# Issuing the stores of P's 16-bit planes from GpSimd's queue

## The chip, the cores and the metric

The kernel runs on one NeuronCore of a Trainium2 chip. The core has five instruction streams that run side by side and meet only at semaphores: TensorE (PE in the profile) multiplies matrices, VectorE (DVE), ScalarE (ACT) and GpSimd (POOL) work on tiles of up to 128 partitions, and SyncE (SP) only issues transfers. Transfers (DMAs) run on 16 DMA engines of the core; an instruction in the queue of SP, ACT or POOL starts one. Each stream takes its instructions strictly in order, so an instruction that waits holds everything behind it in the same stream.

The metric is the time of one execution in microseconds on the device; a kernel's figure is the median of several runs.

## The reference

The inputs are q, k and v of shape (8, 8, 576, 64) and two weight matrices of 512 x 2048 and 2048 x 512. The reference is top-32 attention, then a Fourier mixing block with a small network:

```
scores = (q @ k^T) / 8                       # 64 heads of 576 x 576
kth    = 32nd largest score of each row
P      = softmax(scores where scores >= kth, else -1e9)
x      = P @ v, heads side by side           # (8, 576, 512)
u      = x + real(fft(fft(x, axis=1), axis=2))
un     = (u - mean(u)) / sqrt(var(u) + 1e-6) # over the 512 channels
out    = u + relu(un @ w_ch1) @ w_ch2
```

Everything is computed in float32.

## The kernel before

Heads are taken in 32 pairs, four pairs to each of the 8 batches. The scores of a pair are cut into nine tiles of at most 128 query rows by 576 keys (`IN_PAIR`): four blocks of 128 rows for each of the two heads, and one tile that holds the last 64 rows of both. That makes 288 tiles. The program is written out by hand, one step for each tile i, in the loop at the end of the kernel; there is no scheduler that reorders it. In a step, each engine's instructions for several tiles stand together:

- Scores of tile i + 3: TensorE multiplies (L371 to L404), ScalarE copies them from PSUM to an SBUF tile S, of which there are six.
- The 32 largest scores per row of tile i: VectorE takes four rounds of "eight largest" (MAX8, L425) with three rounds of "replace them" (MATCH_REPLACE8, L427) into a tile wk (`Wk`). A first half of tile i + 1's rounds is mixed in.
- The bound of tile i (`bounds`, L434): one small multiplication on GpSimd writes nt, the negated row maximum and the scaled threshold.
- The mask of tile i - 1 (`mask`, L448 and L451): ScalarE writes a huge number into wk wherever a score lies below the threshold, then GpSimd subtracts this from the scores. The mask needs nt, the subtraction needs the mask.
- The exponential of tile i - 1 (`expo`, L459) on ScalarE.

P @ v needs P with keys on the partitions, that is, transposed. In the first batch, in pair 7 and in the last pair TensorE transposes P (`transposes`, L527). In the other 26 pairs, 234 tiles (`by_dma`), it is done by DMA. There ScalarE writes the exponential into S, and then, two steps after the tile's own, `plane` lets ScalarE split the float32 words into two planes of 16 bits, low halves and high halves (L472, two copies into wk). The planes are stored to a DRAM tile `planes` (L485; for the 64 + 64 row tile two stores, L488). There are 208 stores of 128 rows and 52 of 64 rows. In the next step `turn` (L506) loads the planes back through a transposing DMA into PT, issued by SP; one such load covers a block of both heads. One step after the load's step come the 20 matmuls of P @ v for a chunk of query rows (`attend`, L564), which need all transposing loads of the chunk. Tile wk comes from a pool of three pairs of buffers and is free for a new tile when its store has been read.

Between these, a queue of units of the Fourier block and of the network (`mlp_units`) fills TensorE's time: the matmuls at L755, L812, L816, L966, L993, L1032 and L1163. Around it GpSimd also does the folds ahead of the Fourier step (L651, L678, L719), additions (L839, L1022, L1135) and sums of the network's hidden tiles (L1108). SP also loads q, k and v for coming pairs (L240 to L288), the parts of W2 (L909), and writes the results (L1002, L1059, L1142). The order in each of these streams is that of the program text: in a step `turn`, then the mask, then `plane`, then the units, the loads, the bound, and the rest.

Of the kernel before, what the change touches and what calls it, by code (L numbers as in the profile page):

```python
# [73 lines left out]
def kernel(  # L74
# [9 lines left out]
    nc = tc.nc  # L84
    B, H, S, D = q.shape
# [356 lines left out]
    def by_dma(i):  # L442
        return pair_by_dma(i // PER_PAIR)
# [22 lines left out]
    def plane(i, half):  # L466

        if not (0 <= i < N and by_dma(i)):
            return
        words = Wk[i].bitcast(U16).rearrange("p (h s) -> p h s", h=2)  # L470
        src = Ssb[i].bitcast(U16).rearrange("p (s h) -> p h s", h=2)
        nc.scalar.copy(out=words[:, half, :], in_=src[:, half, :])  # L472
        if half == 0:
            return
        Ssb.pop(i)
        Wk.pop(i)
        pair, t, e = items[i]
        nq = TAIL if e is None else P
        if e != 1:
            planes_of[pair, t] = dramp.tile(  # L480
                [nq, 2, 2 * S], U16, name=f"planes_{pair}_{t}", tag="planes", bufs=3
            )
        to = planes_of[pair, t]
        if e is not None:
            nc.sync.dma_start(out=to[:, :, S * e:S * (e + 1)], in_=words)  # L485
        else:
            for h in range(2):
                nc.sync.dma_start(  # L488
                    out=to[:, :, S * h:S * (h + 1)], in_=words[nq * h:nq * (h + 1)]
                )  # L490
        if e != 1:
            Wp.pop(i)
# [879 lines left out]
    for o, place in ((B12, w2_12), (B21, w2_21)):  # L1372
        at(PER_BATCH + 14, "load2", lambda o=o, place=place: nc.sync.dma_start(
            out=scr[:, o], in_=place
# [117 lines left out]
    while i < N + 5 or plan or queue or sums:  # L1492
# [12 lines left out]
        e = items[j][2] if j < N else None  # L1505
# [57 lines left out]
        if by_dma(i - 1):  # L1563
            mask(i - 1)
        plane(i - 2, 0)
        plane(i - 2, 1)
        run(i, "convert")
        if short:
# [99 lines left out]
```

## Time and profile before

| What | Value |
|---|---|
| median of 3 runs | 1873.34 us (1872.83 to 1874.46) |
| the profiled execution | 1868.68 us, span of the profile 1866.9 us |
| mean granted TensorE clock | 0.955 |
| busy: PE, DVE, ACT, POOL | 1704.1, 1584.9, 1294.6, 912.8 us |
| bytes moved by DMA | 249.16 MB, 133 GB/s on the mean |
| stores of planes from SP | 208 of 288 KB and 52 of 144 KB, 2.7 and 2.6 us from issue to landing |
| transposing loads from SP | 130, 4.6 us from issue to landing |

A profile comes from one execution. Times in it are microseconds from the start of its span. An engine's busy time counts its computing instructions; the issuing of a DMA by an engine's queue does not count as busy. A suffix q (SPq, POOLq) means the queue of that engine: waits and issues. In a list of waits, "SPq L485 <- ACT wk L472: 349.9, 112, 15.4" reads: before its instruction of line 485, SP's queue waited for ScalarE's write to wk in line 472, 349.9 us in all, 112 times, 15.4 us at most. In a timeline a row gives start, duration, engine, line, operation, output<-inputs, shapes, count, and in brackets how long the engine had been idle before it and what ended that. A window's row gives an engine's busy time in a stretch, with the number of instructions behind it. The sizes that the page gives for planes count both the read and the written side.

### The profile page before, as it was taken

How to read it: one execution, taken by the hardware profiler on the slowest of the kernel's cores; microseconds unless marked ns; L12 is line 12 of the kernel's file. 1: busy time of each engine (PE TensorE's matmuls, PEld its weight loads, DVE VectorE, ACT ScalarE, POOL GpSimd, SP SyncE). 2: the span in 40 equal slices, each digit the busy share in tenths (PEclk: the TensorE clock that was granted, in tenths of full speed). 3: DMA queues.
4: the chain of work that ended last, by engine and by line, in shares of the span. 5: the costliest groups of instructions: out<-in, count | busy, mean ns of one | idle time of the engine just before them, and what ended most of it. 6: DMA issues, size and time to landing. Idle time of an engine off the chain costs nothing.

```text
span 1866.9 us, 26900 instructions
## 1 busy us (share of the span) xinstructions
PE 1704.1 (91%) x8134; PEld 1086.8 (58%) x8134; DVE 1584.9 (85%) x3301; ACT 1294.6 (69%) x3104; POOL 912.8 (49%) x1278
## 2 busy tenths in 40 slices
PE   5576699889899999899999999999999999999999
PEld 3344365365456555566556565666567555677677
DVE  7999989889899999999999899999999899762110
ACT  6878659577787778777787688767787678652100
POOL 4768644454745366354644465355545464341012
PEclk7777799899899999999999999999999999999999
DMA  5334016661567755586476755785467655530132
GB/s 168 104 92 115 20 45 162 168 176 26 129 157 202 188 128 130 147 208 160 118 169 169 188 127 139 154 230 133 128 162 189 161 121 146 133 106 6 51 112 72
DMA packets 516576, 249.16 MB, mean 133 GB/s; under 512 B 398288, under 2 KB 506448, under 8 KB 516432
## 3 DMA queue, kind: packets, MB, share of 16 engines
q1 hardware_dynamic: 515664, 247.23, 51.2%
q8 instruction: 65, 1.06, 0.2%
q14 instruction: 79, 0.65, 0.1%
q10 hardware_dynamic: 768, 0.21, 0.1%
HBM read 93.63 MB, written 84.74 MB: 96 GB/s over the span
## 4 chain that ended last, share of the span: by engine, by line
PE 61%; DVE 14%; POOL 7%; ACT 7%; DMA 4%; issue 4%; SPq 1%; POOLq 0%; DVEq 0%
PE hp L966 22%; PE cp L993 8%; PE o L564 7%; DVE m L425 6%; DVE wk L427 6%; PE sp L401 4%; PE cw L1163 4%; PE yp L755 3%; POOL wk L451 3%; PE cv L1163 3%; PE cp L1032 2%; PE sp_t L371 2%; ACT wk L448 1%; DMA PT<-planes 1%; DMA planes<-wk 1%
## 5 line engine op out<-in xcount | busy, mean ns | idle before, releaser
L451 POOL TENSOR_TENSOR wk<-S,wk 128x576 f32<-128x576 f32 x288 | 408.1, 1417 | 524.6 <-ACT wk L448 520.9
L425 DVE MAX8 m<-wk 128x8 f32<-128x576 f32 x864 | 626.8, 750 | 6.2
L966 PE MATMUL hp<-unT,w 128*128 128x256 f32 (+1 forms) x2048 | 528.3, 410 | 5.2 <-ACT unT L884 3.4
L966 PEld LDWEIGHTS hp<-unT,w 128*128 128x128 f32 x2048 | 381.3, 192 | 116.3 <-issue 10.1
L427 DVE MATCH_REPLACE8 wk<-m,wk 128x576 f32<-128x576 f32 x576 | 427.6, 742 | 0.0
L472 ACT COPY wk<-S 128x576 uint16<-128x576 uint16 x468 | 289.4, 669 | 0.0
L448 ACT ACTIVATE wk<-S,nt 128x576 f32<-128x576 f32 x288 | 223.2, 775 | 91.3 <-POOL nt L434 89.8
L564 PE MATMUL o<-PT,v 128*64 128x256 f32 (+3 forms) x1440 | 209.3, 437 | 34.7 <-DMA PT<-planes 18.6
L993 PE MATMUL cp<-w,hT 128*128 128x512 f32 x512 | 236.0, 601 | 0.0
L425 DVE MAX8 m<-S 128x8 f32<-128x576 f32 x288 | 213.8, 742 | 16.1 <-ACT S L375 16.1
L459 ACT ACTIVATE S<-wk,nt 128x576 f32<-128x576 f32 x234 | 184.5, 789 | 51.5 <-POOL wk L451 50.2
L427 DVE MATCH_REPLACE8 wk<-m,S 128x576 f32<-128x576 f32 x288 | 213.7, 742 | 0.0
L970 ACT ACTIVATE hT<-hp 128x320 f32<-128x320 f32 (+1 forms) x256 | 103.2, 411 | 146.0 <-PE hp L966 144.5
L564 PEld LDWEIGHTS o<-PT,v 128*64 128x64 f32 x1440 | 120.3, 160 | 113.4 <-issue 38.9
L401 PE MATMUL sp<-kT,qT 64*128 64x512 f32 (+1 forms) x528 | 169.0, 670 | 15.5 <-ACT S L393 7.7
L404 ACT COPY S<-sp 128x512 f32<-128x512 f32 (+1 forms) x264 | 141.8, 587 | 25.6 <-PE sp L401 24.7
L993 PEld LDWEIGHTS cp<-w,hT 128*128 128x128 f32 x512 | 93.3, 193 | 91.0 <-issue 90.5
L1108 POOL TENSOR_TENSOR hT<-hT 128x512 f32<-128x512 f32 x64 | 81.4, 1275 | 107.5 <-ACT hT L970 91.5
L434 POOL TENSOR_TENSOR nt<-m,cc 128x2 f32<-128x2 f32 x288 | 58.9, 204 | 142.0 <-DVE m L425 139.5
L371 PEld LDWEIGHTS sp_t<-kt,qT 128*128 128x128 f32 x320 | 50.6, 193 | 108.5 <-issue 69.8
L1163 PE MATMUL cw<-w,hT 128*128 128x256 f32 x448 | 104.7, 381 | 1.6 <-issue 1.6
L527 PE MATMUL tpP<-ident,wk 128*128 128x128 f32 x216 | 40.3, 318 | 58.9 <-ACT wk L459 34.1
(160 smaller groups left out, 2178.2 us busy)
## 6 DMA issues: line engine op xcount, KB each, us to landing
planes<-wk SPq DMA_DIRECT2D x208, 288.0 KB, 2.7
w<-w_parts SPq DMA_DIRECT2D x82, 512.0 KB, 4.7
space<-in_moe_w_ch_dram SPq DMA_DIRECT2D x32, 512.0 KB, 3.7
nat<-in_q_dram SPq DMA_DIRECT2D x128, 64.0 KB, 2.5
v<-in_v_dram SPq DMA_DIRECT2D x64, 128.0 KB, 3.0
out_dram<-x SPq DMA_DIRECT2D x32, 256.0 KB, 2.6
nat<-in_k_dram SPq DMA_DIRECT2D x62, 128.0 KB, 3.1
planes<-wk SPq DMA_DIRECT2D x52, 144.0 KB, 2.6
```

Source lines behind the costliest of these rows:

```text
L401: nc.tensor.matmul(sp[r], lhsT=qT[hd, q_cols], rhs=kT[hd, :], start=True, stop=True)
L404: nc.scalar.copy(out=s_t[r, keys], in_=sp[r])
L425: ops.append(lambda src=src, m8=m8: nc.vector.max(out=m8, in_=src))
L427: ops.append(lambda src=src, m8=m8: nc.vector.match_replace(w, m8, src, NEG))
L448: nc.scalar.activation(out=w, in_=Ssb[i], func=AF.Relu, scale=-FAR, bias=Nt[i][:, 1:2])
L451: nc.gpsimd.tensor_tensor(out=w, in0=Ssb[i], in1=w, op=ALU.subtract)
L459: nc.scalar.activation(out=Ssb[i] if by_dma(i) else w, in_=w, func=AF.Exp, bias=Nt.pop(i)[:, 0:1], accum_out=den_t[pair % 3][:, c:c + 1],)
L472: nc.scalar.copy(out=words[:, half, :], in_=src[:, half, :])
L564: nc.tensor.matmul(o[D * e:D * (e + 1), c0:c1], lhsT=vv[:, c, e, :], rhs=pt[:, NF if c == NF else (NF + 1) * e + c, c0:c1], start=(c == 0) ...
L966: nc.tensor.matmul(hp[:, 0:w], lhsT=w1[:, dt, P * it:P * (it + 1)], rhs=unT[:, dt, 0:w], start=(dt == 0), stop=(dt == NDT - 1),)
L993: nc.tensor.matmul(cp, lhsT=hT[:, it, P * n:P * (n + 1)], rhs=w2[:, it, :], start=(it == 0), stop=(it == NIT - 1),)
L1163: nc.tensor.matmul(dst, lhsT=h()[a][:, kc, :], rhs=rhs_of(kc), start=start and kc == 0, stop=kc == NK - 1, skip_group_check=True,)
```

## The change

The two calls in `plane` that issue the stores of the planes are made on GpSimd's queue instead of SP's. Nothing else in the program text differs: the copies at L472 that a store waits for, the tiles, the DRAM buffers, and the transposing loads on SP's queue stay as they are.

```diff
         to = planes_of[pair, t]
         if e is not None:
-            nc.sync.dma_start(out=to[:, :, S * e:S * (e + 1)], in_=words)
+            nc.gpsimd.dma_start(out=to[:, :, S * e:S * (e + 1)], in_=words)
         else:
             for h in range(2):
-                nc.sync.dma_start(
+                nc.gpsimd.dma_start(
                     out=to[:, :, S * h:S * (h + 1)], in_=words[nq * h:nq * (h + 1)]
                 )
```

In the two programs the streams of PE, DVE and ACT hold the same instructions in the same order. In POOL's stream a store of tile i - 2 stands behind the subtraction of tile i - 1 (L451) and ahead of the bound of tile i (L434) and of whatever else POOL has in that step. In SP's stream the stores are gone, and the rest keeps its order.

## The prediction

> **What bounds the kernel now.** I read the page first (busy shares and the chain that ended last), then the waits of SP's queue, then windows of 20 us, then timelines of single tiles.
>
> ```profile
> PE 1704.1 (91%) x8134; PEld 1086.8 (58%) x8134; DVE 1584.9 (85%) x3301; ACT 1294.6 (69%) x3104; POOL 912.8 (49%) x1278
> PE 61%; DVE 14%; POOL 7%; ACT 7%; DMA 4%; issue 4%; SPq 1%; POOLq 0%; DVEq 0%
> ```
>
> TensorE sets the pace, with VectorE close behind. Windows over 240 to 1640 us, where all the stores lie (SP issues them from 237.5 to 1624.3), give PE 1328.90 us busy of 1400 and DVE 1306.59: PE has only 71 us of idle time there, and PE time that a late operand costs is mostly not made up. GpSimd (POOL) is half idle on the mean, but in bursts it is not (busy us and instructions of PE, its weight loads, DVE, ACT and POOL, then the granted clock and the DMA's share and GB/s):
>
> ```profile
> 860.00:960.00 100.00, 98.04 (x493) 60.84 (x492) 97.43 (x202) 81.30 (x198) 63.25 (x108) 1.00 0.55 130
> ```
>
> Hence the timeline of POOL in one tile of that stretch, while a batch's folds (the additions ahead of the Fourier step) run on it:
>
> ```profile
> 911.17 0.19 POOL L434 TENSOR_TENSOR nt<-m,cc 128x2 f32<-128x2 f32 x1
> 912.25 1.41 POOL L451 TENSOR_TENSOR wk<-S,wk 128x576 f32<-128x576 f32 x1 [0.89 <-ACT wk L448]
> ...
> 913.75 1.42 POOL L651 TENSOR_TENSOR fg<-zw 128x254 f32<-128x254 f32 x2
> ...
> 916.94 0.19 POOL L434 TENSOR_TENSOR nt<-m,cc 128x2 f32<-128x2 f32 x1
> ```
>
> The reader should see a ring: nt (L434) lets ACT's mask (L448) start, that lets POOL's subtraction (L451) start, and the next tile's nt stands behind it in POOL's order. Here one turn takes 916.94 - 911.17 = 5.77 us, while VectorE's turn is 5.09 us (its first max of a tile starts at 907.72, 912.80 and 917.89). So in fold steps POOL is already the slowest ring, living on the few us by which tiles run ahead; ACT's timeline shows the price, 2.60 us of idle before the mask at 917.16, released by nt.
>
> On SP's queue the stores hold up, and are held up:
>
> ```profile
> SPq L485 <- ACT wk L472: 349.9, 112, 15.4
> SPq L506 <- DMA planes<-wk: 202.6, 108, 4.4
> ...
> L485 SPq DMA_DIRECT2D planes<-wk x208: 533/560/1454, 237.5 to 1624.3; - x104
> L488 SPq DMA_DIRECT2D planes<-wk x52: 558/584/1587, 281.7 to 1600.9; - x52
> L506 SPq DMA_TRANSPOSE PT<-planes x130: 1294/2538/7724, 256.1 to 1629.1; - x130
> ...
>   PE o L564: 18.6, 8
>   PEld o L564: 4.1, 3
> ```
>
> The last two rows are what PE loses to the path store, transposing load, P @ V: 22.7 us in 11 waits. One of them:
>
> ```profile
> 1030.15 2.46 SPq L506 DMA_TRANSPOSE PT<-planes  x1
> 1032.72 1.22 SPq L488 DMA_DIRECT2D planes<-wk  x2
> 1034.04 1.15 SPq L909 DMA_DIRECT2D w<-w_parts  x2
> 1035.88 1.62 SPq L506 DMA_TRANSPOSE PT<-planes  x1
> ...
> 1041.63 4.61 PE L564 MATMUL o<-PT,v 128*64 128x320 f32 x20 [2.82 <-DMA PT<-planes]
> ```
>
> ACT had finished this tile's words at 1028.7 in its timeline; the store stood 4 us behind loads and another transpose, and PE idled 2.82 us for it.
>
> **The change, part by part.**
>
> *Removed: 260 issues from SP's queue*, 208 x 0.560 + 52 x 0.584 = 147 us, and with them the blocks of 349.9 us in which SP waited for ACT's copies. SP is never busy to the end, so this is worth only what PE gets back of its 22.7 us. In the example the second transpose could start once the loads at L909 are through, 1032.7 + 1.2 = 33.9 instead of 35.88: 2.0 us earlier, of 2.82. Laid beside the timelines, nine of the 52 late P @ V stages with PE waits over 0.5 us are like this (store issued 1.5 to 8.7 us after ACT's copy); each can win up to 2.0 us, less where its wait is shorter. I take a gain of 14 us, with 22.7 as the end. The loads of q, k, v and of W2's parts that stood behind stores start sooner; PE's rows show 1.2 us (L1032) and 3.6 us (L308) of waits for them, so I add nothing.
>
> *Moved: the stores' time of landing.* For the half of the stores that SP issues at once (0.06 us after the copy), POOL is later: its subtraction of the following tile, which comes first in its order, ends 0.35 us after the copy (POOL's against ACT's timeline), and the issue takes X in place of 0.56. The transposing load waits for the landing (108 of 130), so it moves by as much, 0.8 us. Most unheld P @ V stages start 1.3 us or more after their last transpose has landed; about four have under 0.8 us. Loss: 1 us. The wait that the store puts on POOL (for ACT's copy) is over by the time the subtraction ends, so it costs nothing while ACT keeps time; where ACT is late, POOL's next nt is held behind it. VectorE reuses the stored buffer two tiles (10 us) after the store; it shows 0.2 us of waits for landings now.
>
> *Added: 260 issues on POOL, X each.* No row shows POOL issuing a transfer. Below, its cheapest instruction takes 0.19 us (L434). The nearest row is SP's own issue of the same transfer, 0.56; above, the dearest issue in the trace is the transposing load, 2.54 (L506). I start from the nearest row and scale it: over the same 128x576 elements POOL takes 1.417 us (L451) where ACT takes 0.775 (L448) and VectorE 0.742 (L427), a factor of 1.9. X = 0.56 x 1.9 = 1.07 us, in all 278 us, and with 260 stores for 234 tiles 1.2 us per tile. Ends: 0.19 and 2.54.
>
> What it costs: in a 20 us window at VectorE's pace there are 20 / 5.09 = 3.93 tiles. Each needs 1.1 us in which POOL waits for the mask (the 0.89 above and 0.2 for the hand-over) and now 1.2 us of issue: 3.93 x 2.3 = 9.0. What POOL is busy beyond 11.0 us of 20 is lag. Before the change the limit would be 15.7, and only four windows pass it or come within 0.3 of it. Windows of 20 us read on POOL:
>
> ```profile
> 860.00:880.00 20.00, 12.13 (x25) 1.00 0.43 114
> 880.00:900.00 20.00, 13.67 (x23) 1.00 0.65 155
> 900.00:920.00 20.00, 14.20 (x19) 1.00 0.50 114
> 920.00:940.00 20.00, 10.62 (x15) 1.00 0.51 104
> 940.00:960.00 20.00, 12.62 (x27) 1.00 0.67 162
> 960.00:980.00 20.00, 6.22 (x8) 1.00 0.67 180
> ```
>
> Excesses 1.1 + 2.7 + 3.2 - 0.4 + 1.6: the lag climbs to 8.2 us and is gone by 980. The seven stretches of folds, added up in the same way, reach 6.2, 9.5, 5.3, 8.2, 5.5, 5.0 and 6.1, together 46 us. The lag is ACT's too, so S and P come late to PE; covered is what P @ V has in hand, about 1 us in each of the first three stretches and 3 in the last four: 15. Loss: 31 us.
>
> Sum: -14 + 1 + 31 = +18 us on the profiled execution's 1868.7 (span 1866.9 and 1.8 around it). That execution lies 4.7 below the median of the runs, 1873.3; the forecast for the median is 1891.
>
> Two rules of the Trainium skill. "DMA: Bandwidth & Descriptors", section "Latency and other measured facts", puts the first byte of a transfer from SP's or ACT's queue at about 0.6 us, which SP's 0.56 agrees with, and from GpSimd's at about 1 us. X read from that as an estimate is 1.0; the stretches then sum to 38 and the change to about +10.
>
> VectorE's 7 passes per tile over 576 floats take 0.74 us each, 1.3 ns an element. "SBUF — State Buffer", section "Who interferes with whom", speaks against the change if these were two-port operations: each would shut GpSimd out of writing its descriptors. By the same section an operation with one SBUF input outside those modes doesn't; no trace here shows GpSimd issuing beside either. Were it the lock, the time would be that of the second rival.
>
> **Rivals.**
>
> *SP's relief wins (faster).* If X is near SP's 0.56, the limit is 13.2, the stretches sum to 15 us and nearly all is covered: loss about 7, gain 14, 1866. At X = 0.19 with all 22.7 us won back, 1853. For it: ACT idles 31% and POOL 51%, and the waits are there. Against: POOL was slower than its neighbours in every row. It decides below X of about 0.75.
>
> *POOL becomes the bound (much slower).* From the first copy at 236 to the last at 1624 there are 243 tiles, 5.71 us each. POOL's mean per tile is 707.43 / 1400 x 5.71 = 2.89; with 1.1 of waiting and 1.11 X this passes 5.71 at X = 1.55. Beyond it the lag stays: X = 1.9 gives +95 us (1968), X = 2.54 +267 (2140).
>
> *Hidden anyway.* The lag vanishes in slack (DVE waits for PE 150 us in L1121 and L608) and the relief is eaten by another load in SP's order: 1873.
>
> **How the numbers follow.** This kernel's runs spread by 0.09%; a change of 0.2%, 3.7 us, is about what can be told from none. Forecast (X 0.75 to 1.55): 0.42, own range 1876 to 1920. Relief wins: 0.28, 1853 to 1869. POOL bound: 0.23, from 1920. Hidden: 0.07. The range of 8 in 10 leaves out a tenth at each end: 1855 to 1975 (X up to 1.9). Faster 0.28; same 0.08, the hidden case and the forecast's lower edge; slower 0.64.
>
> **What would show it.** Right: POOL's order with a hole or a transfer of 1.0 to 1.2 us behind each L451; ACT's wait for nt (89.8 us in 68) growing to over 200; SP's rows for L485 gone, L506 still waiting on planes; PE's waits for PT gone from the windows where SP was blocked, and new ones near 500, 730, 920, 1130, 1330, 1540. Wrong: X outside 0.75 to 1.55; a landing far later than 2.1 us after the issue ends, which would put every P @ V in wait; or PE finding other work to cover the lag.

## The result and the profile after

| What | Before | After |
|---|---|---|
| median | 1873.23 us | 1898.2 us (1896.79 to 1898.8) |
| ratio, 95% interval | | 1.0138 [1.0122, 1.0153] |
| the profiled execution, its span | 1868.68, 1866.9 us | 1896.79, 1894.7 us |

The change costs 25 us. The forecast was 1891, 18 us over before. The profiled executions differ by 28 us, and the traces are compared on that.

The page of the changed kernel: busy shares; the chain that ended last; the group of the stores, which now counts as POOL's work (busy us, mean ns | idle before it); the two queues that carry the data (packets, MB, share of 16 engines' span); and the stores' time from issue to landing, in us, behind the KB.

```profile
PE 1705.0 (90%) x8134; PEld 1087.8 (57%) x8134; DVE 1584.8 (84%) x3301; ACT 1295.6 (68%) x3104; POOL 1092.0 (58%) x1538
...
q1 hardware_dynamic: 451600, 178.21, 38.4%
q0 software_dynamic: 19136, 69.03, 10.8%
...
PE 58%; POOL 12%; ACT 11%; DVE 7%; DMA 4%; issue 4%; SPq 2%; POOLq 0%; DVEq 0%; ACTq 0%
...
L485 POOL DMA_DIRECT2D planes<-wk x208 | 144.1, 693 | 38.6 <-POOL wk L451 21.9
...
planes<-wk POOLq DMA_DIRECT2D x208, 288.0 KB, 2.9
planes<-wk POOLq DMA_DIRECT2D x52, 144.0 KB, 3.7
```

No other engine is busy for more than 1 us longer; POOL is busy 179 us longer, since the page counts the issuing of a store as POOL's work. The chain has lost PE and DVE (61 to 58%, 14 to 7%) and gained POOL and ACT (7 to 12%, 7 to 11%): the ring of bound, mask and subtraction decides more often. ACT's waits say the same (us in all, times, longest; the kernel before, then the changed one):

```profile
ACT wk L448 <- POOL nt L434: 89.8, 68, 4.0
```
```profile
ACT wk L448 <- POOL nt L434: 131.2, 84, 5.0
```

The timeline of POOL shows one turn of the ring, in the fold step that answers to the one shown of before:

```profile
926.67 0.27 POOL L434 TENSOR_TENSOR nt<-m,cc 128x2 f32<-128x2 f32 x1
927.82 1.41 POOL L451 TENSOR_TENSOR wk<-S,wk 128x576 f32<-128x576 f32 x1 [0.89 <-ACT wk L448]
929.44 0.68 POOL L485 DMA_DIRECT2D planes<-wk  x1 [0.20 <-POOL wk L451]
930.05 0.28 POOL L654 COPY fg<-zw 128x4 f32<-128x4 f32 x1
930.20 1.48 POOL L651 TENSOR_TENSOR fg<-zw 128x254 f32<-128x254 f32 x2
...
933.39 0.21 POOL L434 TENSOR_TENSOR nt<-m,cc 128x2 f32<-128x2 f32 x1
```

From bound to bound it takes 933.39 - 926.67 = 6.72 us, where it took 5.77. The store's own row is 0.68 us, it starts 0.20 us after the subtraction has ended, and some small instructions behind it are slower (L434's mean rose from 204 to 256 ns). Together that is 0.95 us in this turn.

PE's waits for P transposed (PT) did not shrink. The rows of the planes and of PT that answer to those of before:

```profile
L485 POOL DMA_DIRECT2D planes<-wk x208: 645/684/847, 237.6 to 1652.7; - x104
L506 SPq DMA_TRANSPOSE PT<-planes x130: 1273/2455/9973, 267.6 to 1657.3; - x130
L488 POOL DMA_DIRECT2D planes<-wk x52: 575/614/667, 282.9 to 1629.4; - x52
...
  PE o L564: 31.7, 9
...
  PEld o L564: 5.7, 1
```

The last two rows add to 37.4 us, where they added to 22.7, but such a sum counts stops twice. PEld is PE's weight load, and here both halted together: its 5.7 us are one stop that stands in PE's row too, at 291.65, and so do most of the 4.1 us of before (at 288.44 and 942.03). PE's row alone went from 18.6 us in 8 waits to 31.7 in 9. The page's row for all matmuls of P @ v, before and after, has PE's idle time ahead of them whatever is named as its end:

```profile
L564 PE MATMUL o<-PT,v 128*64 128x256 f32 (+3 forms) x1440 | 209.3, 437 | 34.7 <-DMA PT<-planes 18.6
```
```profile
L564 PE MATMUL o<-PT,v 128*64 128x256 f32 (+3 forms) x1440 | 209.5, 438 | 44.0 <-DMA PT<-planes 26.2
```

That is 9.3 us of the 27 us by which PE idles longer. Where the rest is lost stands behind e12 and e13. SP's largest wait is now the one for the stores' landing:

```profile
SPq L506 <- DMA planes<-wk: 676.2, 117, 45.1
```

### The profile page after: what moved, and what is told of

Read it like the earlier page. It is cut to its first block, busy times and chain, and to the rows that moved or that the text cites. A ratio compares the mean times of both kernels' runs of the same rounds, so it can differ in the third digit from the quotient of the medians.

```text
span 1894.7 us, 26963 instructions
## 1 busy us (share of the span) xinstructions
PE 1705.0 (90%) x8134; PEld 1087.8 (57%) x8134; DVE 1584.8 (84%) x3301; ACT 1295.6 (68%) x3104; POOL 1092.0 (58%) x1538
## 3 DMA queue, kind: packets, MB, share of 16 engines
q1 hardware_dynamic: 451600, 178.21, 38.4%
q0 software_dynamic: 19136, 69.03, 10.8%
## 4 chain that ended last, share of the span: by engine, by line
PE 58%; POOL 12%; ACT 11%; DVE 7%; DMA 4%; issue 4%; SPq 2%; POOLq 0%; DVEq 0%; ACTq 0%
PE hp L966 22%; PE o L564 7%; PE cp L993 4%; PE sp L401 4%; PE cw L1163 4%; POOL wk L451 4%; PE cv L1163 3%; DVE m L425 3%; DVE wk L427 3%; PE cp L1032 3%; ACT wk L448 3%; PE yp L755 2%; ACT wk L472 2%; POOL fg L651 2%; PE sp_t L371 2%
## 5 line engine op out<-in xcount | busy, mean ns | idle before, releaser
L451 POOL TENSOR_TENSOR wk<-S,wk 128x576 f32<-128x576 f32 x288 | 409.6, 1422 | 441.8 <-ACT wk L448 441.6
L472 ACT COPY wk<-S 128x576 uint16<-128x576 uint16 x468 | 289.1, 668 | 0.0
L564 PE MATMUL o<-PT,v 128*64 128x256 f32 (+3 forms) x1440 | 209.5, 438 | 44.0 <-DMA PT<-planes 26.2
L564 PEld LDWEIGHTS o<-PT,v 128*64 128x64 f32 x1440 | 119.9, 159 | 122.7 <-issue 52.5
L485 POOL DMA_DIRECT2D planes<-wk x208 | 144.1, 693 | 38.6 <-POOL wk L451 21.9
L434 POOL TENSOR_TENSOR nt<-m,cc 128x2 f32<-128x2 f32 x288 | 73.7, 256 | 64.9 <-DVE m L425 64.4
```

Source lines behind the costliest of these rows:

```text
L451: nc.gpsimd.tensor_tensor(out=w, in0=Ssb[i], in1=w, op=ALU.subtract)
L485: nc.gpsimd.dma_start(out=to[:, :, S * e:S * (e + 1)], in_=words)
L564: nc.tensor.matmul(o[D * e:D * (e + 1), c0:c1], lhsT=vv[:, c, e, :], rhs=pt[:, NF if c == NF else (NF + 1) * e + c, c0:c1], start=(c == 0) ...
```

## The experiments

To see where time arises, I compare the starts of the P @ v stages in two traces: how much later each starts than in the kernel before. The columns are stretches between such starts, named by their time in the trace before; each cell is the time lost in that stretch, in us. Stretches marked F hold a batch's folds.

| Kernel | 225 to 453 | F 453 to 564 | 564 to 864 | F 864 to 942 | F 1119 to 1169 | F 1323 to 1371 | F 1527 to 1582 | the three gaps between | all, at 1694 |
|---|---|---|---|---|---|---|---|---|---|
| changed | 6.3 | 6.9 | -0.9 | 5.0 | 2.5 | 2.6 | 2.1 | 3.7 | 27.9 |
| e1 | 3.4 | 6.1 | 1.1 | 4.3 | 4.2 | 2.4 | 3.6 | 2.3 | 27.6 |
| e7 | 1.8 | 1.5 | 0.4 | -0.1 | 3.8 | 0.0 | -1.5 | 2.2 | 5.6 |
| e8 | 6.2 | 9.6 | 0.0 | 4.8 | 5.8 | 4.3 | 3.9 | 2.5 | 34.5 |
| e12 | 6.4 | 8.0 | 2.2 | 1.6 | 1.6 | 0.0 | -2.0 | 3.8 | 20.0 |

(Small shifts before 225 and after 1582 are left out of the stretches.) Each cell compares one execution with one other. In the trace of e11, below, whose median is within 3 us of before, the cells of the fold stretches reach 4.4 us, so a single cell of a few us says little. Below, theory A is that the loss is POOL's occupied time in the ring; theory B that it comes from SP's queue running free.

**e1: POOL's time without the change.** Stores back on SP; a scratch addition takes the store's place on POOL.

```diff
-            nc.gpsimd.dma_start(out=to[:, :, S * e:S * (e + 1)], in_=words)
+            nc.sync.dma_start(out=to[:, :, S * e:S * (e + 1)], in_=words)
...
+        for _ in range(4 if e is None else 2):
+            nc.gpsimd.tensor_tensor(out=idle_t, in0=idle_t, in1=idle_t, op=ALU.add)
```

> The stores stay on SP's queue as in the kernel before; where the change puts a store into POOL's order, POOL instead adds a small scratch tile to itself, twice 128x126 elements for a store of 128 rows and four times for the 64 + 64 row tile (about 0.46 us each by POOL's rows for that size, 0.9 us in all, against the 0.68 us of the store's row and the 0.2 us before it). Theory A: the loss is POOL's occupied time in the ring bound - mask - subtraction; then this alone costs 18 to 28 us over before (1891 to 1901). Theory B: the loss comes from SP's queue running free, its loads colliding with stores and transposing loads, and POOL's time is hidden; then this stays within 4 us of before.

Measured: 1896.58 against 1870.87 us, ratio 1.0141 [1.0113, 1.0169]. That is the changed kernel's ratio without a single store moved. ACT's wait and POOL's row for the scratch addition (two in one row):

```profile
ACT wk L449 <- POOL nt L435: 128.6, 80, 4.6
```
```profile
927.98 0.86 POOL L493 TENSOR_TENSOR idle<-idle 128x126 f32<-128x126 f32 x2
```

Theory B, as the cause of the whole loss, falls; about 0.9 us per store on POOL is enough for all of it. In the turn that was shown of the changed kernel these additions cost 0.82 us where the store cost 0.95. The table shows the loss in the same stretches, within its noise.

**e2 and e5: SP held back again.** e2 is the changed kernel with a small transfer at each old place of a store in SP's order; e5, run later as its control, is the kernel before with the same addition.

```diff
+        mark = dramp.tile([16, 32], U16, name=f"mark_{i}", tag="mark", bufs=8)
+        nc.sync.dma_start(out=mark, in_=words[0:16, 1, 0:32])
```

> The changed kernel, and at each place where a store stood in SP's order SP issues a transfer of 1 KB that waits for the same copy of ScalarE, so that SP's loads are held back as they were before. Theory A: no better than the changed kernel, 1893 to 1900, as POOL's part is untouched. Theory B: the loads no longer run ahead, PE's waits for PT go from 37 back to about 23 us and the time to under 1882.

> The kernel before, with the 1 KB transfer of e2 added on SP's queue behind each tile's stores: the control for e2. If the 234 transfers are free in themselves, this stays within 5 us of before, and the 18 us by which e2 exceeds the changed kernel are the price of SP being held while POOL's stores land later. If they cost by themselves (SP's queue 103 us longer, its loads later), this is 10 to 20 us above before and e2 says nothing on the order of SP's queue.

Measured: e2 1914.35 us, ratio 1.0229 [1.0204, 1.0255]; e5 1880.02 us, 1.0053 [1.0037, 1.007]. Holding SP back did not help, against theory B; but it also cost 16 us more than the changed kernel, which neither theory expected. The control says that 0.5%, 9.5 us, of that is the added transfers themselves. The 7 us that remain are too near the size of the control's own effect to be read as the price of SP's order. I count the pair as inconclusive on that. PE's wait for PT, which theory B put back at 23 us, is 39.1 us in e2's row.

**e3: the stores on ScalarE's queue.**

```diff
-            nc.gpsimd.dma_start(out=to[:, :, S * e:S * (e + 1)], in_=words)
+            nc.scalar.dma_start(out=to[:, :, S * e:S * (e + 1)], in_=words)
```

> The stores are issued from ScalarE's queue, right behind the copies that they wait for: SP's queue is as free as in the changed kernel, POOL has nothing added, ScalarE has 0.56 us per store (147 us in all, it idles 30%). Theory A: freeing SP neither wins nor loses much; 1868 to 1880, what is above 1873 being ScalarE's issue time. Theory B: the free SP queue costs as much as in the changed kernel, 1890 to 1900. My forecast's gain term, were it real, would show here as 1855 to 1865.

Measured: 1910.7 us, ratio 1.0201 [1.0175, 1.0227]. Neither expectation held: it is the dearest place of the three. ACT's timeline shows what each store costs it:

```profile
708.17 1.24 ACT L472 COPY wk<-S 128x576 uint16<-128x576 uint16 x2
709.45 0.56 ACTq L485 DMA_DIRECT2D planes<-wk  x1
710.05 1.51 ACT L393 COPY S<-sp 64x256 f32<-64x256 f32 x4 [0.63 <-ACT wk L472]
```

ACT stands still for 0.63 us between its copies and its next work. POOL is relieved (911.4 us busy, as before), SP is free, and the stores land soonest of all: on the mean the transposing load has landed 8.7 us after ACT's copy, where it was 8.9 before and 9.6 in the changed kernel. It is slower all the same, so what these sooner landings win is less than what ACT's time costs. That ACT's lost time reaches PE through its copies of scores is argued, not shown.

**e4: twice POOL's time.** The changed kernel with e1's scratch additions behind each store.

> The changed kernel with the scratch additions of e1 behind each store, so that POOL's added time per store is about 1.8 us in place of 0.9. Theory A with the forecast's arithmetic: 1.11 x 1.8 = 2.0 us per tile, 2.89 + 1.1 + 2.0 = 6.0 us against 5.71 per tile, so POOL is the bound on the mean and the lag no longer goes away: 68 us or more over before, 1935 to 1965, and ScalarE waits for nt over 300 us. If the cost is only linear: 1923. Theory B: as the changed kernel, 1893 to 1903.

Measured: 1950.83 us, ratio 1.0419 [1.0393, 1.0446], 80 us over before where the single dose costs 25.

```profile
ACT wk L449 <- POOL nt L435: 212.3, 136, 5.6
```

The time lies in the window of the ring's arithmetic and above twice the single dose. ACT's wait grew less than I had written. The cost is more than linear, as "POOL becomes the bound" has it. That POOL is then the bound throughout is not shown: it still waits 374.4 us for ACT's masks, and by the starts of the P @ v stages 47 of the 84 us lost lie in the five F stretches.

**e7 and e8: where POOL's time costs.** POOL issues only outside the fold stretches (e7), or only in them (e8); SP issues the other stores.

```diff
+        store = nc.sync if 2 <= (i + 2) % PER_BATCH < 17 else nc.gpsimd   # e7; e8 exchanges the two
-            nc.gpsimd.dma_start(out=to[:, :, S * e:S * (e + 1)], in_=words)
+            store.dma_start(out=to[:, :, S * e:S * (e + 1)], in_=words)
```

> Stores from POOL only in the steps in which POOL has no folds or their followers (steps 17 to 37 of each batch's 36, 129 of 234 tiles), from SP in the others. Theory A, lag in the fold stretches: nearly all of the loss is gone, within 5 us of before (1868 to 1878). Rival C, POOL's time costs the same wherever it stands, as ScalarE's did in e3: 129/234 of 25, 14 us over before.

> The complement of e7: stores from POOL only in steps 2 to 16 of each batch (105 of 234 tiles), where the folds and, in the first of these stretches, W1's and W2's differences run on POOL; from SP in the others. Theory A: nearly the whole loss, 20 to 28 us over before. Rival C: 105/234 of 25, 11 us.

Measured: e7 1874.19 against 1870.52 us, ratio 1.0017 [1.0002, 1.0033]; e8 1901.9 us, ratio 1.0174 [1.0149, 1.0199]. 129 of the 234 tiles cost 4 us on POOL, the other 105 cost everything: theory A's place, and rival C (the same price everywhere) falls. e8's median is even above the full change's, but the two intervals touch. ACT's waits tell them apart; the first row is e7's, the second e8's:

```profile
ACT wk L448 <- POOL nt L434: 91.5, 73, 3.8
```
```profile
ACT wk L448 <- POOL nt L434: 119.4, 69, 4.6
```

**e9 and e10: SP's relief alone.** Stores on SP as before; from the second batch on the six loads of q that stand ahead of the 64 + 64 row tile's stores come two steps later (e9) or one (e10).

```diff
-            if i % PER_PAIR == 5:
+            if i < PER_BATCH and i % PER_PAIR == 5:
                 load_nat("q", pair_of + 2)
             if i % PER_PAIR == 7:
                 load_v(pair_of + 1)
+                if i >= PER_BATCH:
+                    load_nat("q", pair_of + 2)
```

> The kernel before, stores on SP, but from the second batch on the loads of q for a coming pair (six issues, 3.3 us of SP's queue) stand two steps later, behind the stores of the 64 + 64 row tile and not ahead of them: SP's relief at the one place where PE waits, without any time on POOL. If the forecast's gain term holds (the store issued 2 us sooner reaches PE), PE's waits for PT fall from 23 to about 12 us and the time to 1860 to 1868. If the transposing loads land no sooner, since they then share the DMA engines with the loads that stood behind, it is within 4 us of before.

> As e9, but the loads of q stand one step later than before, not two: behind the store of the 64 + 64 row tile, ahead of its transposing load, which waits for the store's landing anyway. If e9's loss came from q landing late (PE waited 17 us for it), that is gone and what e9 won at PT (23 to 10 us) is mostly kept: 1860 to 1868. If the time stays above before by 5 us or more, e9's loss is not q's lateness but the loads' meeting with the transposing loads on the DMA engines.

Measured: e9 1886.25 against 1870.52 us, ratio 1.0094 [1.007, 1.0118]; e10 1884.2 against 1871.48, ratio 1.007 [1.0056, 1.0084]. Both slower. PE's waits for DMAs, of e9 and then of e10:

```profile
PE tpq L308 <- DMA nat<-in_q_dram: 17.0, 13, 4.1
...
PE o L564 <- DMA PT<-planes: 9.9, 7, 5.3
...
PE cp L1032 <- DMA w<-w_parts: 9.4, 4, 3.5
```
```profile
PE o L564 <- DMA PT<-planes: 23.6, 11, 4.6
PE tpq L308 <- DMA nat<-in_q_dram: 4.2, 1, 4.2
```

In e9 the wait for PT fell as forecast (18.6 to 9.9 in this row), and the waits for q and for W2's parts, 3.6 and 1.2 before, took its place and more. In e10 q is in time again and the wait for PT is back: the 64 + 64 row tile's store is issued 0.8 us sooner on the mean than before (2.1 against 2.9 us after ACT's copy), yet its transposing load has landed 10.0 us after the copy, where it was 9.5, since that load now stands behind the q loads in SP's order. What is won for one transfer is taken from its neighbours. Taken together these rows are 13 us above before in e9, which lost 16; e10's 13 us they do not explain, and these stay open.

**e11: only the 64 + 64 row tile's stores on POOL.**

```diff
             for h in range(2):
-                nc.sync.dma_start(
+                nc.gpsimd.dma_start(
```

> The changed kernel's move for the 52 stores of the 64 + 64 row tiles alone; the 208 others stay on SP. POOL gets 26 x 1.5 us, 11 of the 26 in fold stretches: by theory A a loss of 1 to 4 us. The wait for PT that the move was to shorten is this tile's: if the forecast's gain term were right, a net gain of 8 to 13 us (1857 to 1863); if the transposing load lands no sooner for it, within 4 us of before.

Measured: 1868.61 against 1871.48 us, ratio 0.9982 [0.9971, 0.9992]. This is the only version that is faster than the kernel before, by 3 us. It is no proof of the gain term: PE's wait for PT is not shorter,

```profile
PE o L564 <- DMA PT<-planes: 22.3, 9, 6.3
```

and its profiled span, 1867.0, is that of before, 1866.9. Where its 3 us come from, the profile does not show.

**e12 and e13: the same work in another place of POOL's order.** The store is issued behind the step's bound, in the fold stretches (e12) or everywhere (e13).

```diff
+        def store():
+            ...
+        if 2 <= (i + 2) % PER_BATCH < 17:      # e13: always
+            after_bound.append(store)
+        else:
+            store()
...
         bounds(i)
+        for fn in after_bound:
+            fn()
+        after_bound.clear()
```

> The changed kernel, but in steps 2 to 16 of each batch (the fold stretches) POOL issues a tile's store behind that step's bound (L434) and not ahead of the folds and the bound; elsewhere as in the changed kernel. POOL's work is the same, but the store then falls into the 0.9 us in which POOL waits for ScalarE's mask. Theory A, the ring: the bound is no longer late by the store, most of the 20 to 28 us of the fold stretches is gone: 1872 to 1884, with ScalarE's wait for nt back from 131 to under 105 us. What stays above before is the store's later landing (2.5 to 4 us later in these steps). If POOL's occupied time as such is what costs, or the later landing costs as much as the ring did: 1890 to 1900.

> As e12, with all 260 stores behind the step's bound. Outside the fold stretches the bound waits for VectorE, so these stores go out 1 to 2 us later than in e12. e7 puts the stores' cost there near zero; if the transposing loads have the 2 to 3 us in hand that the timelines show, this equals e12 within 5 us; if landing times decide, PE's waits for PT grow past 40 us and it is 5 to 15 us above e12.

Measured: e12 1893.11 against 1871.53 us, ratio 1.0116 [1.0094, 1.0138]; e13 1898.07, ratio 1.0141 [1.0115, 1.0168]. POOL's timeline of e12, the same turn of the ring:

```profile
926.60 0.18 POOL L434 TENSOR_TENSOR nt<-m,cc 128x2 f32<-128x2 f32 x1
926.73 0.64 POOL L487 DMA_DIRECT2D planes<-wk  x1
927.68 1.40 POOL L451 TENSOR_TENSOR wk<-S,wk 128x576 f32<-128x576 f32 x1 [0.30 <-ACT wk L448]
...
932.37 0.18 POOL L434 TENSOR_TENSOR nt<-m,cc 128x2 f32<-128x2 f32 x1
```

The turn is back at 932.37 - 926.60 = 5.77 us, exactly what it was before: the store has slipped into POOL's wait for the mask, which shrank from 0.89 to 0.30 us. ACT's wait for the bound and PE's wait for PT in e12:

```profile
ACT wk L448 <- POOL nt L434: 89.2, 69, 3.8
```
```profile
PE o L571 <- DMA PT<-planes: 44.2, 13, 6.8
```

So the ring is repaired, and the table shows it: the four fold stretches from 864 on lose 1.2 us together in place of 12.2. But the whole gains little (the intervals of e12 and of the change overlap), since the other price has risen: on the mean the stores go out 1.8 us after ACT's copy in place of 0.9 (2.7 in place of 0.8 in the steps that were changed), and PE waits 44.2 us for PT in place of 26.2. Most of e12's loss, 14.4 of 20 us, lies before 564. In the kernel before, the stages of P @ v at 490, 517, 544 and 564 us started 0.1, 1.4, 1.6 and 0.7 us after their last load had landed, so they had little in hand. My expectation named this term and took it for small; that was wrong. e13, with all stores later still, is 5 us above e12, which the intervals do not tell apart.

PE's idle time ahead of its matmuls (us, from the four traces) shows the two prices side by side:

| PE's idle time ahead of | Before | Changed | e1 | e12 |
|---|---|---|---|---|
| P @ v (L564) | 34.7 | 44.0 | 39.7 | 63.6 |
| transposes of q and k (L308) | 12.1 | 21.8 | 18.3 | 4.7 |
| the Fourier step (L755, L812, L816) | 5.2 | 16.9 | 16.0 | 4.1 |
| all its matmuls | 158.9 | 186.0 | 177.8 | 173.0 |

The lag of the ring reaches PE mostly through late copies of ACT and late folds of POOL, in the second and third row: with the ring's loss they rise (changed, e1), with the ring repaired they are gone (e12). The later stores of e12 stand in the first row. PE was also busy 9 us longer in e1 and 6 in e12, though only 1 in the changed kernel; no run tells why.

## Why the prediction was right or wrong

**The sign and the mechanism were right; that the size came so near is in part luck.** The forecast was +18 us, measured +25. The mechanism, a lag of POOL that climbs in the fold stretches because the store stands between the subtraction and the next bound, is shown by four runs: e1 makes the loss without moving a store, e8 puts it into the fold stretches and e7 empties the rest, e12 gives the ring its old turn by order alone. But X, the time per issue, was taken too large and a gain was counted that did not come, and the two made up for each other. By the prediction's own windows, an X of 0.95 gives seven stretches that sum to 34 us in place of 46, 19 after the 15 that were covered, and a change of -14 + 1 + 19 = +6; with the issue's own row, 0.68, its arithmetic falls on the side of the first rival.

**The issue, taken as 1.07 us, is 0.68,** plus 0.20 us of idle time ahead of it and slower neighbours behind it: 0.95 us in the ring. Scaling SP's 0.56 by POOL's slowness was too much for the row, which lies outside the 0.75 to 1.55 of the forecast, a sign of being wrong that the prediction had named; what the ring feels lies inside. POOL's busy time rose by 179 us, not 278.

**The lag's price, taken as 31 us, is about 26** by e1, which has this term alone. The forecast's stretches are those of the table. The subtraction of what P @ v has in hand was crude: the two early stretches lose 13 of 28 us, and the later ones 2 to 5 each. ACT's wait for the bound was forecast at over 200 us; it is 131. The idle that I expected between the ring's members was partly there before. Nor did PE's new waits for PT come near the six times that were named: in the changed kernel only the one at 499 us does, with 0.3 us, and the ring's lag costs PE more ahead of other matmuls (the table behind e12). A small misreading: by the prediction's own limit the lag of the stretch that it shows is still 3.5 us at 980.

**The step that failed is the gain of 14 us from SP's relief.** With it and the 1 us of later landing, the change would have to cost 13 us less than e1, which has the ring's term alone. The ratios are 1.0138 and 1.0141, half a microsecond apart, with some 6 us either way; that e1's additions are a little shorter than the store makes up for some 4 us. The growth of PE's waits for PT is no measure of this step, since e1, which relieves nothing, has 25.8 us in the row that was 18.6. Its upper end was also misread: the 22.7 us count some stops on both PE and PEld, and PE's own row was 18.6.

The first half of the step was right. For the 64 + 64 row tile, the one I showed, the last store is issued 1.2 us after ACT's copy, where it was 2.9. But it lands only 0.7 us sooner (4.9 against 5.6), its transposing load is issued 0.4 us sooner, and that has landed no sooner at all (9.6 against 9.5, means over 26 tiles). The example itself, in the changed kernel:

```profile
1050.38 1.08 SPq L909 DMA_DIRECT2D w<-w_parts  x2
1051.56 2.31 SPq L506 DMA_TRANSPOSE PT<-planes  x1
```
```profile
1060.50 5.21 PE L564 MATMUL o<-PT,v 128*64 128x320 f32 x20 [4.84 <-DVE m L425]
```

The landing of this transposing load, before and then in the changed kernel (one load, so the three numbers are the same):

```profile
DMA to landing us min/median/max: 5.5/5.5/5.5
```
```profile
DMA to landing us min/median/max: 8.8/8.8/8.8
```

As forecast, the load is issued as soon as the loads of L909 are through, 6.0 us after ACT's copy where it was 7.2. But it takes 8.8 us to its landing where it took 5.5, and PE waits 4.84 us where it waited 2.82. (The row names DVE as the end of this wait; the load had landed just 0.1 us before.) One batch later, the load takes 9.2 us where it took 6.6, and PE waits 4.99 us where it waited 2.40:

```profile
1269.19 4.97 PE L564 MATMUL o<-PT,v 128*64 128x320 f32 x20 [4.99 <-DMA PT<-planes]
```

In both places the next tile's large store, which on SP's queue went out 1.7 and 3.2 us behind this load, goes out from POOL 0.3 and 0.65 us behind it, and takes 8.4 and 8.3 us to land where the median is 2.9. Three loads of W2's parts stood ahead in the second place before as well. I had reckoned with the queue's order alone, not with what transfers in flight together do to each other; which neighbour makes the load late, no run separates. e9 and e10 say the same from the other side.

**The later landing, taken as 1 us,** cannot be separated from the relief in the change itself: together they come to nothing within the 6 us that the intervals allow. e12 shows that this term can be large. VectorE's wait for a landed store, which I left out, came once, with 7.6 us where it was 0.2.

**The rivals.** "Relief wins" fell with the gain term. "POOL becomes the bound" agrees with e4, which at about 1.8 us per store is 80 us over before, where the arithmetic had at least 68 and a linear price 50; the threshold of 1.55 itself no run tests. "Hidden anyway" nearly holds for the tiles outside the fold stretches (e7, 4 us).

**The skill's rules.** The estimate from "DMA: Bandwidth & Descriptors" ("Latency and other measured facts"), 1.0 us per issue, was nearer to the ring's 0.95 than my 1.07; the +10 us that I worked out from it is too low because the same gain of 14 stands in it. The page speaks of the first byte of a transfer, which no row here times; the rows of 0.56 us on SP and 0.68 us on POOL are the issuing. The port rule of "SBUF — State Buffer" ("Who interferes with whom") showed no sign of a lock: over 208 stores beside VectorE's passes the issue took 0.645 to 0.847 us.

## What to carry to other kernels

An engine that is half idle on the mean can still be the slowest member of a ring, and there an instruction put between two members can cost its full length, as here 0.95 us in a turn of 5.77; read busy time per stretch, and set it beside the waits within the ring, not beside the span. The same instruction is nearly free a place further on, where its engine waits for another member anyway, but a transfer that goes out later needs slack at its consumer. And a relieved queue is worth nothing until the transfer has landed sooner: what it lets through is in flight beside it.

## What was not expected of the hardware

- A store issued from POOL moves in fewer packets: 64064 packets of the SP queue's (515664 - 451600) are replaced by 19136 for the same data. The DMA engines' share hardly changed (51.2% before, 38.4 + 10.8 after).
- From issue to landing the small stores took 3.7 us from POOL against 2.6 from SP, the large ones 2.9 against 2.7 (medians). Part of the path that was won in issuing is lost there.
- In 107 of the 208 large stores POOL idled 0.2 us between its subtraction and the store (21.9 us in all), which the profile puts down to POOL's own subtraction; why the other stores show no such wait is open.
- A store issued from ACT's queue stops ACT for 0.6 us in the row shown, and this cost more time (e3, 2.0%) than POOL's 0.95 us did (1.4%).
